# Moving the softmax sums, the place bases and the first weight splits of a fused attention and mixture-of-experts kernel

## The chip, the cores and the metric

The kernel runs on one core of a Trainium2 chip. The metric is the device time of one execution in microseconds (us), lower is better; for a kernel it is the median of several runs. The engines are PE (TensorE: matmuls and transposes, with PEld its weight loads), DVE (VectorE), ACT (ScalarE), POOL (GpSimd) and SP (SyncE, which only issues transfers). Each takes its own instructions strictly in the order in which the program lists them, and engines wait for one another by semaphores.

## What is computed

Causal attention with a window of 64 over q, k, v of shape (8, 8, 576, 64), and then a mixture of eight experts, of which each token takes one, over the 4608 rows of 512 that it gives:

```python
scores = scale * np.matmul(q, k.transpose(0, 1, 3, 2))          # scale = 1/sqrt(64)
mask = (rel >= 0) & (rel < 64)                                   # rel = query - key
attn = np.exp(np.where(mask, scores, -1e9) - max)
attn = attn / (np.sum(attn, axis=-1, keepdims=True) + 1e-09)
x = (attn @ v) as rows of (B * S, H * D)                         # 4608 x 512
logits = normalized(x) @ normalized(expert_emb).T / tau
expert_idx = np.argmax(logits, axis=1)
gate_w = softmax(logits)[expert_idx]
out[mask_e] = gate_w * (np.maximum(x[mask_e] @ w1[e], 0.0) @ w2[e])   # for each of 8 experts
```

## The kernel before

The program has a manual schedule: instructions are issued in the order in which the Python code is written, and no scheduler moves them. It has three stretches.

**Attention, stages 0 to 34.** The tokens are 36 tiles of 128 rows. `stages(s)` (L520) is one turn of a software pipeline: it computes the scores of tile s, the weighted values of tile s - 2 and the routing of tile s - 3. In one turn PE does `scores(s)` (L215), for groups of four tiles that end three tiles back also `logits_four` (L351), then `values_other(s-2)` (L275) into the only PSUM tile `pair`, `attn_transposes(s-1)` (L245), `x_transposes(s-3)` (L331), at some turns `ranks` (L412 to L416), and `values_mine(s-2)` (L289), which completes `pair`. ACT copies scores (`own_scores`, L222), the turned attention (`attn_copy`, L255) and the turned x (`xT_evac`, L337) out of PSUM, squares x with an accumulator (`squares`, L324), triggers the load of a k tile (L176) and takes the exponentials (L236). DVE masks the scores (`all_scores`, L225), takes maxima (L229), masks the turned attention (`attn_prev`, L258), and then runs `x_out` (L309): it adds 1e-9 to the row sums in `pair` (L313), inverts them (L314) and multiplies the 512 columns of `pair` by them into x (L315). Only then is `pair` free, so the next turn's L275 waits for L315. POOL subtracts the maxima (L233), masks the other half of the attention (L261) and scatters finished rows of x into a DRAM table sorted by expert (`place`, L462).

At some turns DVE also routes a group. `choose(G)` (L382) has five small operations on the group's logits, which ACT has copied out of PSUM into the rows of x (`four_out`, L361). `ranks(G)` counts on PE, in PSUM, how many earlier tokens took the same expert; `rank_rows(G)` (L440) then adds each expert's base in the table (L445), masks by the choice (L447), sums (L450) and casts (L453) to give each token's row in the table.

**The first expert's weights.** Matmuls of the expert layers run as three products of two-part numbers (a high part and the rest), so w1 and w2 are split: ACT makes the high part and DVE the rest. During attention the first expert's w1 is loaded in eight halves (`wsteps`, stages 8 to 28) and split in eight halves (`wsplit`, stages 13 to 32, L600 on ACT and L601 on DVE, at the end of the stage). After stages 32 and 33 `x_parts` prepares the first two slots of 128 table rows for that expert: four 32-column turns on DVE (L770), the high part on ACT (L781), the rest on POOL (L785). Their loads (L755) are issued after stage 30.

**The mixed stretch and the experts.** After stage 34 the last tile's attention is woven by hand with the first expert's first layer (L887). Tile 35's parts are called one by one (L1091 to L1211). Then DVE computes from the counts which expert each slot of rows belongs to (`slot_rows`), and `step(g)` runs one slot group after another: layer 1 (L887), layer 2 (L947), splits of the next weights (L158, L161), scatter of results (L959).

Of the kernel before, what the change touches and what calls it, by code (L numbers as in the profile page):

```python
# [9 lines left out]
F32 = mybir.dt.float32  # L10
# [73 lines left out]
def attention_moe(ctx, tc, q, k, v, emb, tau, w1, w2, kc, kt, out):  # L84
# [56 lines left out]
    upper = const.tile([P, P], BF16, name="upper")  # L141
    ones = const.tile([P, P], BF16, name="ones")
    half = const.tile([P, 1], F32, name="half")
    embT = ap.tile([P, 4, 32], F32, name="embT", bufs=1)
    xs = dram.tile([TBL, ROW], F32, name="xs")

# [27 lines left out]
    def load_k(T, engine=nc.sync):  # L174
        if T < NT:
            engine.dma_start(kT[:, T % RK * KT:(T % RK + 1) * KT], k[T])  # L176
# [43 lines left out]
    def own_scores(T):  # L220
        sm[T] = ap.tile([P, 4, 2, WIN], F32, name="sm", bufs=3)
        nc.scalar.copy(sm[T], sv[:, :, :, 1])  # L222
# [12 lines left out]
    def exponentials(T):  # L235
        nc.scalar.activation(sm[T], sm[T], AF.Exp, scale=0.125)  # L236
# [65 lines left out]
    def x_rows(a, b):  # L302

        if a // 4 in (2, 5):
            return xmore[:, a % 4:a % 4 + b - a]
        i = a if a < 8 else a - 12 if a < 20 else a - 24 if a < 34 else a - 34
        return xall[:, i:i + b - a]

    def x_out(T):  # L309
        t = xr[T] = x_rows(T, T + 1)[:, 0]  # L310
        p4 = px.pop(T)[:, :, :4 * (D + 1)].rearrange("p b (h d) -> p b h d", h=4)
        sums = ap.tile([P, 2, 2, 4], F32, name="sums")
        nc.vector.tensor_scalar(out=sums[:, 0], in0=p4[:, :, :, D], scalar1=1e-9, scalar2=None, op0=ALU.add)  # L313
        nc.vector.reciprocal(sums[:, 1], sums[:, 0])  # L314
        nc.vector.tensor_tensor(out=t[:, :DM].rearrange("p (b c d) -> p b c d", b=2, c=4), in0=p4[:, :, :, :D],  # L315
                                in1=sums[:, 1].unsqueeze(3).to_broadcast([P, 2, 4, D]), op=ALU.mult)
# [55 lines left out]
    def in_rows(G):  # L372

        return x_rows(*GROUPS[G])[:, :, C_LOG:C_LOG + E]
# [6 lines left out]

    def choose(G):  # L382

        L = in_rows(G)
        a, b = GROUPS[G]
        n = b - a
        m = ap.tile([P, n, 1], F32, name="m")
        c8 = ap.tile([P, n, E], F32, name="c8")
        oh = ohs[G] = ap.tile([P, n, E], BF16, name="oh")
        sh = [P, n, E]  # L390
        nc.vector.reduce_max(out=m, in_=L, axis=AX.X)
        nc.vector.tensor_tensor(out=c8, in0=L, in1=m.to_broadcast(sh), op=ALU.is_equal)
        nc.vector.tensor_tensor(out=c8, in0=c8, in1=cs[:, K_DESC:K_DESC + E].unsqueeze(1).to_broadcast(sh), op=ALU.mult)
        nc.vector.reduce_max(out=m, in_=c8, axis=AX.X)
        nc.vector.tensor_tensor(out=oh, in0=c8, in1=m.to_broadcast(sh), op=ALU.is_equal)
# [11 lines left out]
    def ranks(G):  # L407

        a, b = GROUPS[G]
        n = b - a  # L410
        rank[G] = rkb[0][:, 64:128].rearrange("p (a g e) -> p a g e", a=2, e=E)[:, G % 2, :n]
        nc.tensor.matmul(rank[G], lhsT=upper, rhs=ohs[G], start=True, stop=False)  # L412
        for i in range(1, n):
            nc.tensor.matmul(rank[G][:, i:], lhsT=ones, rhs=ohs[G][:, i - 1:i].to_broadcast([P, n - i, E]), start=False, stop=False)
        for i in range(4):
            nc.tensor.matmul(rank[G], lhsT=ones, rhs=before[G][:, i:i + 1].to_broadcast([P, n, E]), start=False, stop=i == 3)  # L416

    late = [const.tile([P, E], F32, name=f"late{i}") for i in range(len(CUTS))]
    shift = [const.tile([P, 1], F32, name=f"shift{i}") for i in range(len(CUTS))]
# [20 lines left out]
    def rank_rows(G):  # L440
        a, b = GROUPS[G]
        n = b - a
        rk = ap.tile([P, n, E], F32, name="rk")
        at = [cs[:, K_E:K_E + E], *late][sum(a >= cut for cut in CUTS)]
        nc.vector.tensor_tensor(out=rk, in0=rank.pop(G), in1=at.unsqueeze(1).to_broadcast([P, n, E]), op=ALU.add)  # L445
        yield
        nc.vector.tensor_tensor(out=rk, in0=rk, in1=ohs.pop(G), op=ALU.mult)  # L447
        yield
        pos = ap.tile([P, n], F32, name="pos")
        nc.vector.reduce_sum(out=pos, in_=rk, axis=AX.X)  # L450
        yield
        rks[G] = ap.tile([P, n], I32, name="pi")
        nc.vector.tensor_copy(rks[G], pos)  # L453
        yield
# [47 lines left out]


    wsteps = {}
    for i, s0 in enumerate((8, 10, 15, 18, 21, 24, 26, 28)):
        c, h = divmod(i, 2)
        at = slice(h * 512, (h + 1) * 512)
        wsteps.setdefault(s0, []).append(lambda c=c, at=at: nc.sync.dma_start(out=w1raw[c][:, at], in_=w1v[0, :, c, at]))

    for i, s0 in enumerate((29, 30, 30, 31, 31, 32, 32, 33)):  # L510
        c, h = divmod(i, 2)
        wsteps.setdefault(s0, []).append(lambda c=c, h=h: nc.sync.dma_start(out=w2raw[c][:, h], in_=w2v[0, :, c, h]))
    wsplit = {s0: (i // 2, slice(i % 2 * 512, i % 2 * 512 + 512)) for i, s0 in enumerate((13, 15, 20, 23, 26, 28, 30, 32))}

    def warm(n, to=back):

# [3 lines left out]
    def stages(s):  # L520

        def there(d):
            return 0 <= s - d < NT

        def ending(d):
            return [G for G, (a, b) in enumerate(GROUPS) if b + d == s]
# [7 lines left out]
        if s < 3:  # L534
            warm(12, misc)
        own_scores(s)
        if there(4) and s - 4 >= 28:
            logits(s - 4)
        four = [G for G in ending(3) if len(range(*GROUPS[G])) == 4]
# [33 lines left out]
        if there(3):  # L573
            squares(s - 3)
        load_k(s + RK - 1, nc.scalar)
        if s > 3:
            attn_prev(s - 1)
            attn_own(s - 1)
        if there(2):
            x_out(s - 2)  # L580
        if 0 < s <= 3:
            turned()
            attn_prev(s - 1)
            attn_own(s - 1)
# [4 lines left out]
        for G, (a, b) in enumerate(GROUPS):  # L589
            for T in range(a, b):  # L590
                if s == (T + 9 if b - a == 4 else b + 4):
                    place(T)
        for G in ending(3):
            choose(G)
            tokens(G)
            count(G)
        exponentials(s)
        if s in wsplit:
            c, at = wsplit[s]
            nc.scalar.copy(w1h[c][:, at], w1raw[c][:, at])  # L600
            nc.vector.tensor_tensor(out=w1l[c][:, at], in0=w1raw[c][:, at], in1=w1h[c][:, at].bitcast(F32), op=ALU.subtract)  # L601
# [449 lines left out]
    nc.vector.memset(ones, 1.0)  # L1051
    nc.vector.memset(low, -BIG / 64)
    nc.vector.memset(half, 0.5)
    nc.scalar.copy(shift[0], half)
    nc.vector.memset(embT, 0.0)
    nc.vector.memset(before[0], 0.0)
# [10 lines left out]
    for t in range(NT - 1):  # L1067
        stages(t)
        if t == 0:
            nc.vector.tensor_copy(upper, xbuf[2][:, :P])  # L1070
        if t == 1:
            expert_norms()
        if t == 2:
            expert_emb()
        if t == 3:
            expert_emb_T()
        if t == CUTS[0] + 4:
            sum_counts(CUTS[0])
            begin_late(0, counts("early"))
        if t == 30:  # L1080
            load_x(0)
            load_x(1)
        if t in (32, 33):
            x_parts(t - 32)

    stage_t.close()
    rkb[0] = misc
# [206 lines left out]
```

## Time and profile before

| what | value |
|---|---|
| median of 3 runs | 628.08 us (627.51 to 628.99) |
| the profiled execution's own time | 623.06 us |
| its span, first to last instruction | 621.3 us |
| granted TensorE clock, mean | 0.994 |
| PE, PEld busy | 594.8 us (96%), 530.9 us (85%) |
| DVE, ACT, POOL busy | 426.9, 354.9, 231.4 us |
| the same, 100 to 120 us (attention): PE, DVE, ACT, POOL of 20 us | 17.24, 17.72, 13.22, 15.81 |
| the same, 240 to 260 us (experts) | 20.00, 13.38, 12.60, 5.50 |

Rows of a timeline read: start in us, duration in us, engine, line, operation, output<-inputs, count, and in brackets how long the engine had been idle before and which instruction ended that. Rows of groups read: line, engine, operation, tiles, shape, count | busy us, mean ns of one | idle before, and who ended it. A queue name such as SPq or ACTq is the engine's issue of a transfer, not busy time.

### The profile page before, as it was taken

The page shows a single profiled execution, that of the slowest core. Times are in us where ns is not written, and L with a number is a line of the kernel's source. Part 1 is how long each engine was busy: PE and PEld are TensorE (multiplying, and loading weights), DVE is VectorE, ACT ScalarE, POOL GpSimd, SP SyncE. Part 2 cuts the span into 40 slices and gives each one's busy share as a digit, 9 for nine tenths or more (in the row PEclk, how much of TensorE's full clock was granted, in tenths as well). Part 3 has the DMA queues.
Part 4 walks back from the last instruction along what each step waited for, and adds up shares of the span by engine and source line. Part 5 has one row for each costly group of instructions (what it writes and reads, how often), then busy time and mean ns, then how long its engine had stood idle before and what let it go on. Part 6 is the DMA issues. An engine that isn't in the chain of part 4 may idle for free. (4 is left out here: it accounts for less than half of the span.)

```text
span 621.3 us, 17783 instructions
## 1 busy us (share of the span) xinstructions
PE 594.8 (96%) x6836; PEld 530.9 (85%) x6836; DVE 426.9 (69%) x883; ACT 354.9 (57%) x566; POOL 231.4 (37%) x224
## 2 busy tenths in 40 slices
PE   8899989888999999999999999999999999999996
PEld 8777777777899898989988999899889998998884
DVE  2778888887778657675566776656765677657623
ACT  2676766676542447466466664645676476636533
POOL 1567877778733133213203331142023331222011
PEclk9999999999899999999999999999999999999998
DMA  8878888886335588886786897849777976775351
GB/s 293 263 208 256 259 264 270 266 273 186 151 115 204 137 271 279 255 257 227 250 269 219 273 299 245 258 157 324 252 242 240 283 275 206 241 273 199 111 167 37
DMA packets 85789, 143.75 MB, mean 231 GB/s; under 512 B 15797, under 2 KB 36021, under 8 KB 85696
## 3 DMA queue, kind: packets, MB, share of 16 engines
q1 hardware_dynamic: 74560, 112.87, 58.5%
q0 software_dynamic: 6000, 19.18, 7.8%
q10 hardware_dynamic: 5136, 10.49, 5.0%
q8 instruction: 55, 0.90, 0.6%
q14 instruction: 38, 0.31, 0.2%
HBM read 123.23 MB, written 20.05 MB: 231 GB/s over the span
## 5 line engine op out<-in xcount | busy, mean ns | idle before, releaser
L887 PE MATMUL ph<-xh,w1l 128*128 128x256 f32 x576 | 162.3, 282 | 1.0 <-DVE w1l L161 1.0
L887 PE MATMUL ph<-xh,w1h 128*128 128x256 f32 x576 | 162.4, 282 | 0.0
L887 PE MATMUL ph<-xl,w1h 128*128 128x256 f32 x576 | 161.7, 281 | 0.0
L959 POOL DMA_INDIRECT out<-o,rest x39 | 49.4, 1266 | 220.4 <-ACT o L956 204.8
L947 PE MATMUL po<-w2h,hh 128*128 128x512 f32 x312 | 122.3, 392 | 0.0
L947 PE MATMUL po<-w2h,hl 128*128 128x512 f32 x312 | 121.9, 391 | 0.0
L947 PE MATMUL po<-w2l,hh 128*128 128x512 f32 x312 | 121.7, 390 | 0.0
L901 DVE SCALAR_TENSOR_TENSOR hl<-ph,hh 128x512 fp32r<-128x512 f32 x78 | 53.4, 689 | 93.0 <-ACT hh L897 92.9
L161 DVE TENSOR_TENSOR w2l<-w2raw,w2h 128x1024 fp32r<-128x1024 f32 x80 | 94.7, 1220 | 24.6 <-ACT w2h L158 22.9
L887 PEld LDWEIGHTS ph<-xh,w1l 128*128 128x128 f32 x576 | 108.4, 188 | 1.6 <-DVE w1l L161 1.4
L887 PEld LDWEIGHTS ph<-xl,w1h 128*128 128x128 f32 x576 | 108.6, 188 | 0.8
L887 PEld LDWEIGHTS ph<-xh,w1h 128*128 128x128 f32 x576 | 108.2, 188 | 0.8
L158 ACT CAST w2h<-w2raw 128x1024 fp32r<-128x1024 f32 x80 | 81.5, 1048 | 40.0 <-PE po L947 28.7
L161 DVE TENSOR_TENSOR w1l<-w1raw,w1h 128x1024 fp32r<-128x1024 f32 x76 | 89.2, 1236 | 11.0 <-ACT w1h L158 11.0
L785 POOL TENSOR_TENSOR xl<-xt,xh 128x512 fp32r<-128x512 f32 x37 | 47.8, 1293 | 101.2 <-ACT xh L781 101.2
L897 ACT ACTIVATE hh<-ph 128x512 fp32r<-128x512 f32 x78 | 46.1, 595 | 57.2 <-PE ph L887 50.6
L158 ACT CAST w1h<-w1raw 128x1024 fp32r<-128x1024 f32 x76 | 73.9, 1047 | 0.0
L947 PEld LDWEIGHTS po<-w2h,hl 128*128 128x128 f32 x312 | 58.6, 188 | 12.5
L947 PEld LDWEIGHTS po<-w2h,hh 128*128 128x128 f32 x312 | 58.6, 188 | 11.5
L947 PEld LDWEIGHTS po<-w2l,hh 128*128 128x128 f32 x312 | 58.6, 188 | 11.4
L781 ACT CAST xh<-xt 128x512 fp32r<-128x512 f32 x39 | 24.2, 620 | 57.4 <-DVE xt L770 56.6
L233 POOL TENSOR_TENSOR sm<-sm,st 128x512 f32<-128x512 f32 x36 | 37.4, 1040 | 37.8 <-DVE st L229 29.8
(194 smaller groups left out, 834.5 us busy)
## 6 DMA issues: line engine op xcount, KB each, us to landing
w2raw<-in_w SPq DMA_DIRECT2D x76, 512.0 KB, 5.8
w1raw<-in_w SPq DMA_DIRECT2D x72, 512.0 KB, 4.7
xb<-xs SPq DMA_DIRECT2D x156, 64.0 KB, 6.2
v<-in_v SPq DMA_DIRECT2D x36, 260.0 KB, 4.2
qT<-in_q SPq DMA_DIRECT2D x36, 256.0 KB, 4.1
kT<-in_k ACTq DMA_DIRECT2D x32, 256.0 KB, 4.1
w1raw<-in_w SPq DMA_DIRECT2D x8, 256.0 KB, 4.3
w2raw<-in_w SPq DMA_DIRECT2D x8, 256.0 KB, 4.7
```

What stands on the lines that cost most here:

```text
L158: nc.scalar.copy(hi[c], raw[c])
L161: eng.tensor_tensor(out=lo[c], in0=raw[c], in1=hi[c].bitcast(F32), op=ALU.subtract)
L233: nc.gpsimd.tensor_tensor(out=t, in0=t, in1=st.pop(T).unsqueeze(2).to_broadcast([P, 8, WIN]), op=ALU.subtract)
L781: nc.scalar.copy(xh, t)
L785: eng.tensor_tensor(out=xl, in0=t, in1=xh.bitcast(F32), op=ALU.subtract)
L887: nc.tensor.matmul(o, lhsT=ww[c][:, f * P:(f + 1) * P], rhs=xx[:, c, :n], start=(c == 0 and i == 0), stop=(c == 3 and i == 2))
L897: nc.scalar.activation(hh, ph[g, part], AF.Relu)
L901: nc.vector.scalar_tensor_tensor(out=hl, in0=ph.pop((g, part)), scalar=0.0, in1=hh.bitcast(F32), op0=ALU.max, op1=ALU.subtract)
L947: nc.tensor.matmul(po[a], lhsT=xx[:, f, at], rhs=ww[f // 2][:, f % 2], start=(f == 0 and i == 0), stop=(f == 7 and i == 2))
L959: d = nc.gpsimd.indirect_dma_start(out=out, out_offset=bass.IndirectOffsetOnAxis(ap=tok, axis=0), in_=o, in_offset=None, bounds_check=N - ...
```

## The change

1. **Sums on ACT.** The addition of 1e-9 to the eight row sums of a tile (L313 on DVE) becomes an ACT activation, `Identity` with a bias read from a constant [128, 1] tile. In the stages it is listed on ACT behind `squares` and the k load, ahead of the exponentials; DVE keeps the inversion and the multiplication. For tiles 33 to 35, in the mixed stretch, it is listed where `x_out` is called.
2. **Bases on PE.** The experts' bases are added by one more matmul at the end of `ranks`, a single row of ones (fp32) against the bases. `rank_rows` loses its addition; its mask now reads PSUM.
3. **Choice from PSUM.** For groups of four, `choose` reads the logits from PSUM instead of the copy in the rows of x. The copy is still made, since the rows carry it.
4. **Even steps.** The eight w1 loads move to stages 8, 10, 12, 15, 17, 19, 21, 23 and the splits to 14, 16, ..., 28.
5. **Turned x.** The two `x_parts` after stages 32 and 33 are taken apart and put inside those stages.

```diff
+    def x_sums(T):
+        sums = sums_of[T] = ap.tile([P, 2, 2, 4], F32, name="sums")
+        p4 = px[T][:, :, :4 * (D + 1)].rearrange("p b (h d) -> p b h d", h=4)
+        nc.scalar.activation(sums[:, 0], p4[:, :, :, D], AF.Identity, bias=tiny)
+
     def x_out(T):
+        if T not in sums_of:
+            x_sums(T)
+        sums = sums_of.pop(T)
...
-        nc.vector.tensor_scalar(out=sums[:, 0], in0=p4[:, :, :, D], scalar1=1e-9, scalar2=None, op0=ALU.add)
         nc.vector.reciprocal(sums[:, 1], sums[:, 0])
...
     def choose(G):
-        L = in_rows(G)
+        L = plq[:, G % 2, :, :E] if n == 4 else in_rows(G)
...
     def ranks(G):
         for i in range(4):
-            nc.tensor.matmul(rank[G], lhsT=ones, rhs=before[G][:, i:i + 1].to_broadcast([P, n, E]), start=False, stop=i == 3)
+            nc.tensor.matmul(rank[G], lhsT=ones, rhs=before[G][:, i:i + 1].to_broadcast([P, n, E]), start=False, stop=False)
+        at = [cs[:, K_E:K_E + E], *late][sum(a >= cut for cut in CUTS)]
+        nc.tensor.matmul(rank[G], lhsT=one, rhs=at[:1].unsqueeze(1).to_broadcast([1, n, E]), start=False, stop=True)
...
     def rank_rows(G):
-        nc.vector.tensor_tensor(out=rk, in0=rank.pop(G), in1=at.unsqueeze(1).to_broadcast([P, n, E]), op=ALU.add)
-        yield
-        nc.vector.tensor_tensor(out=rk, in0=rk, in1=ohs.pop(G), op=ALU.mult)
+        nc.vector.tensor_tensor(out=rk, in0=rank.pop(G), in1=ohs.pop(G), op=ALU.mult)
...
-    for i, s0 in enumerate((8, 10, 15, 18, 21, 24, 26, 28)):
+    for i, s0 in enumerate((8, 10, 12, 15, 17, 19, 21, 23)):
...
-    wsplit = {s0: (i // 2, slice(i % 2 * 512, i % 2 * 512 + 512)) for i, s0 in enumerate((13, 15, 20, 23, 26, 28, 30, 32))}
+    wsplit = {s0: (i // 2, slice(i % 2 * 512, i % 2 * 512 + 512)) for i, s0 in enumerate((14, 16, 18, 20, 22, 24, 26, 28))}
...
     def stages(s):
         own_scores(s)
+        if s == 33:
+            x_hi(0)
...
         load_k(s + RK - 1, nc.scalar)
+        if there(2):
+            x_sums(s - 2)
...
         if there(2):
             x_out(s - 2)
+        if s in (32, 33):
+            x_turned(s - 32)
...
+        if s == 33:
+            x_lo(0)
         for G in ending(3):
             choose(G)
...
         exponentials(s)
+        if s == 33:
+            x_hi(1)
+            x_lo(1)
...
-        if t in (32, 33):
-            x_parts(t - 32)
```

How the instructions move, on the engines and at the places that matter below. First ACT in a stage in the middle of the attention: `score`, `back` and `xback` are the PSUM tiles of scores, turned attention and turned x, `sq` the discarded squares, `sm` the scores in SBUF. Before:

```order
L337 COPY xfour<-xback 128x512
L324 ACTIVATE sq,xmore<-xmore 128x512
L176 DMA kT<-in_k 128x512
L236 ACTIVATE sm<-sm 128x512
L222 COPY sm<-score 128x512
```

and in the changed kernel:

```order
L347 COPY xfour<-xback 128x512
L334 ACTIVATE sq,xr<-xr 128x512
L178 DMA kT<-in_k 128x512
L316 ACTIVATE sums<-pair,tiny 128x8
L238 ACTIVATE sm<-sm 128x512
L224 COPY sm<-score 128x512
```

The sums, which read `pair`, now stand on ACT between the k load and the exponentials, in each of the stages.

Second, DVE in stage 32 and the start of stage 33, where the first turned x (`xt`) is made. Before:

```order
L313 TENSOR_SCALAR sums<-pair 128x8
L314 RECIPROCAL sums<-sums 128x8
L315 TENSOR_TENSOR xr<-pair,sums 128x512
L601 TENSOR_TENSOR w1l_112<-w1raw,w1h_108 128x512
L770 STREAM_TRANSPOSE xt_224<-xb_218 128x4x32 x4
L225 COPY_PREDICATED sm<-cs,score 128x512
```

and now:

```order
L325 TENSOR_TENSOR xr<-pair,sums 128x512
L790 STREAM_TRANSPOSE xt_228<-xb_222 128x4x32 x4
L227 COPY_PREDICATED sm<-cs,score 128x512
L231 TENSOR_REDUCE st<-sm 128x8
L260 TENSOR_TENSOR aM<-back,cs 128x512
L324 RECIPROCAL sums<-sums 128x8
L325 TENSOR_TENSOR xr<-pair,sums 128x512
L790 STREAM_TRANSPOSE xt_229<-xb_223 128x4x32 x4
L456 TENSOR_TENSOR rk<-rkb,oh 128x32
```

The split is gone from stage 32, and the second tile's turns stand ahead of the stage's rank and choice operations instead of behind them.

Third, ACT around the last tile's output in the mixed stretch (`hh` is the first expert's hidden layer, `w2h` the high part of its w2). Before:

```order
L337 COPY xT<-back 128x512
L324 ACTIVATE sq,xr<-xr 128x512
L897 ACTIVATE hh_3369<-ph_3416 128x512
L158 CAST w2h_3363<-w2raw_103 128x1024
L337 COPY xT<-back 128x512
```

and now:

```order
L347 COPY xT<-back 128x512
L334 ACTIVATE sq,xr<-xr 128x512
L917 ACTIVATE hh_3373<-ph_3420 128x512
L160 CAST w2h_3367<-w2raw_105 128x1024
L316 ACTIVATE sums<-pair,tiny 128x8
L347 COPY xT<-back 128x512
```

The last tile's sums stand behind a cast of 1024 columns.

More of the change, by code (lines that the diff above doesn't have):

```diff
@@ L143, in attention_moe @@
     half = const.tile([P, 1], F32, name="half")
+    tiny = const.tile([P, 1], F32, name="tiny")
+    one = const.tile([1, P], F32, name="one")
     embT = ap.tile([P, 4, 32], F32, name="embT", bufs=1)
@@ L307, in x_rows @@
         return xall[:, i:i + b - a]
+    sums_of = {}
+    def x_sums(T):
+        sums = sums_of[T] = ap.tile([P, 2, 2, 4], F32, name="sums")
+        p4 = px[T][:, :, :4 * (D + 1)].rearrange("p b (h d) -> p b h d", h=4)
+        nc.scalar.activation(sums[:, 0], p4[:, :, :, D], AF.Identity, bias=tiny)
     def x_out(T):
+        if T not in sums_of:
+            x_sums(T)
+        sums = sums_of.pop(T)
         t = xr[T] = x_rows(T, T + 1)[:, 0]
         p4 = px.pop(T)[:, :, :4 * (D + 1)].rearrange("p b (h d) -> p b h d", h=4)
-        sums = ap.tile([P, 2, 2, 4], F32, name="sums")
-        nc.vector.tensor_scalar(out=sums[:, 0], in0=p4[:, :, :, D], scalar1=1e-9, scalar2=None, op0=ALU.add)
         nc.vector.reciprocal(sums[:, 1], sums[:, 0])
@@ L443, in rank_rows @@
         rk = ap.tile([P, n, E], F32, name="rk")
-        at = [cs[:, K_E:K_E + E], *late][sum(a >= cut for cut in CUTS)]
-        nc.vector.tensor_tensor(out=rk, in0=rank.pop(G), in1=at.unsqueeze(1).to_broadcast([P, n, E]), op=ALU.add)
-        yield
-        nc.vector.tensor_tensor(out=rk, in0=rk, in1=ohs.pop(G), op=ALU.mult)
+        nc.vector.tensor_tensor(out=rk, in0=rank.pop(G), in1=ohs.pop(G), op=ALU.mult)
         yield
@@ L1053, in attention_moe @@
     nc.vector.memset(half, 0.5)
+    nc.vector.memset(tiny, 1e-9)
+    nc.vector.memset(one, 1.0)
     nc.scalar.copy(shift[0], half)
```

## The prediction

> **What bounds the kernel now.** I read the 20 us stretches first, because the share of busy time mixes two regimes, and then what PE waited for in each.
>
> ```profile
> 100.00:120.00 20.00, 17.24 (x492) 14.66 (x484) 17.72 (x46) 13.22 (x31) 15.81 (x16) 1.00 0.83 270
> 240.00:260.00 20.00, 20.00 (x127) 18.08 (x126) 13.38 (x20) 12.60 (x16) 5.50 (x5) 1.00 0.79 241
> PE pair L275 <- DVE xr L315: 9.9, 17, 1.3
> PE ph L887 <- DVE w1l L161: 1.0, 2, 0.5
> ```
>
> The columns after each stretch are PE, PEld, DVE, ACT and POOL. The experts (second row) are bound by PE, which never pauses; after 160 us its largest sum of waits is the last row, 1.0 us in two pieces. So whatever the change saves ahead of 163 us, when the first expert layer starts, should arrive at the end, and PE time added later is paid in full. In attention no engine is full; PE waits above all (third row, up to 160 us) for the multiplication L315, which frees `pair`. I therefore follow one stage (17) from L275 to the next L275.
>
> ```profile
> 80.31 0.70 PE L275 MATMUL pair<-v,aM 64*64 64x65 f32 x32 [1.32 <-DVE xr L315]
> 80.91 0.73 DVE L225 COPY_PREDICATED sm<-cs,score 128x512 f32<-128x512 uint32 x1 [0.66 <-ACT sm L222]
> 81.97 0.25 PE L416 MATMUL rkb<-before,ones 128*128 128x32 bf16 x4
> 82.16 1.05 PE L289 MATMUL pair<-v,aM 64*128 64x65 f32 x24
> 82.21 0.33 ACTq L176 DMA_DIRECT2D kT<-in_k  x1
> 82.35 0.68 DVE L258 TENSOR_TENSOR aM<-back,cs 128x512 f32<-128x512 f32 x1
> 82.59 0.64 ACT L324 ACTIVATE sq<-xr 128x512 bf16<-128x512 f32 x1
> 83.12 0.20 ACT L324 ACTIVATION_READ_ACCUMULATOR sq<-xr 128x1 f32 x1
> 83.28 0.17 DVE L313 TENSOR_SCALAR sums<-pair 128x8 f32<-128x8 f32 x1 [0.24 <-PE pair L289]
> 83.48 0.20 DVE L314 RECIPROCAL sums<-sums 128x8 f32<-128x8 f32 x1
> 83.72 0.69 DVE L315 TENSOR_TENSOR xr<-pair,sums 128x512 f32<-128x512 f32 x1
> 84.33 0.18 DVE L445 TENSOR_TENSOR rk<-rkb,cs 128x32 f32<-128x32 f32 x1
> 84.46 0.70 PE L275 MATMUL pair<-v,aM 64*64 64x65 f32 x32 [0.38 <-DVE xr L315]
> 88.98 0.70 PE L275 MATMUL pair<-v,aM 64*64 64x65 f32 x32
> 93.05 0.68 PE L275 MATMUL pair<-v,aM 64*64 64x65 f32 x16 [0.38 <-DVE xr L315]
> 97.14 0.46 PE L275 MATMUL pair<-v,aM 64*64 64x65 f32 x16 [0.74 <-DVE xr L315]
> ```
>
> PE needs 2.90 us from L275 to the end of L289 (83.21); then come addition, inversion and multiplication, and L275 follows at 4.15. This round, through PE and DVE, sets the stage. Stage 18 takes 4.52 without a wait: PE has a group's logits to do before L275, and is itself the limit. Stages 19 and 20 take 4.07 and 4.09. The four make 16.83 us. Stages with a split or a blocked choice are longer:
>
> ```profile
> 29.16 0.70 PE L275 MATMUL pair<-v,aM 64*64 64x65 f32 x32 [0.38 <-DVE xr L315]
> 150.65 0.70 PE L275 MATMUL pair<-v,aM 64*64 64x65 f32 x32 [0.37 <-DVE xr L315]
> L447 DVE TENSOR_TENSOR rk<-rk,oh 128x32 f32<-128x32 f32 x7 | 3.3, 476 | 0.2
> ```
>
> The first two rows are 28 stages (5 to 33) apart: 121.5 us, against 7 x 16.83 = 117.8. So late DVE work costs some 3.7 us now. That is all that relieving DVE can win here.
>
> **The change part by part: the stages.** DVE loses L313 (0.20 from its start to the next) in every stage, and for every group L445 (0.21). L447, 476 ns on average, becomes an operation with one input from PSUM, like L445's 0.18, though it does the same work on the same shape; it is one with both inputs in SBUF that is long. The Trainium skill (SBUF — State Buffer, Who interferes with whom) says that a `tensor_tensor` with both inputs in SBUF contends with GpSimd's reads; the trace agrees, 0.48 against 0.18. In `choose`, though, the operation behind the one that now reads PSUM has two SBUF inputs (L393) and would inherit the block, so I count nothing for it. DVE's round (multiplication to next operation 0.61, L225 to L258 1.44, L258 0.68, inversion 0.24) is then 2.97 us; with five choice operations, each 0.20 to 0.24 like L313 and L314, it is 4.1, with a split (0.69, row below) 3.7. None is above the 4.15, and with splits in even stages and choices in odd ones they never add up. So rounds of PE, and of ACT, cover DVE's, and I take its lateness as gone; were the cover away, up to the 3.7 us would be.
>
> But ACT's answer comes later than DVE's would. ACT's accumulator read, behind the copies and the squares, starts 2.81 us after L275 (83.12). What the sums cost follows from these rows of groups and of the last tile:
>
> ```profile
> L897 ACT ACTIVATE hh<-ph 128x512 fp32r<-128x512 f32 x78 | 46.1, 595 | 57.2 <-PE ph L887 50.6 <-PE ph L933 6.3
> L956 ACT ACTIVATE o<-po,gate 128x512 f32<-128x512 f32 x38 | 24.0, 681 | 0.9 <-DVE gate L844 0.7 <-ACTq L1031 0.2
> L545 ACT COPY xr<-misc 128x16 f32<-128x16 f32 x1 | 0.2, 175 | 0.0
> 181.33 0.19 ACT L324 ACTIVATION_READ_ACCUMULATOR sq<-xr 128x1 f32 x1
> 181.42 0.59 ACT L897 ACTIVATE hh<-ph 128x512 fp32r<-128x512 f32 x1
> 181.90 1.04 ACT L158 CAST w2h<-w2raw 128x1024 fp32r<-128x1024 f32 x1
> 181.96 0.17 DVE L313 TENSOR_SCALAR sums<-pair 128x8 f32<-128x8 f32 x1 [1.13 <-PE pair L289]
> 183.50 0.49 PE L331 MATMUL back<-cs,xr 128*128 128x128 f32 x3
> ```
>
> The instruction behind an accumulator read starts 0.09 after it. A small copy from PSUM takes 175 ns; an activation with an operand per partition (L956's scale; the sums' bias is of that kind) takes 86 ns more than one without (L897). I take 0.26 us, between 0.175 and 0.29. So the sums end 2.81 + 0.09 + 0.26 = 3.16 after L275, the inversion starts at 3.19, the multiplication 0.24 later, L275 0.74 after that: 4.17 for a plain stage, 4.26 where ACT also copies a group's logits (one small instruction, 0.09 like the one above). In rank stages PE is last: 2.90, plus the new matmul, plus 0.03 + 0.26 + 0.03 + 0.24 + 0.74. The matmul is not in the trace; the nearest row is L416, four bf16 ones in 0.25 together, the later ones some 0.03 apart. A single row of fp32 could cost anything from one such step, 0.03, to as much as all four, 0.25; I take 0.12, the middle. That makes 4.32. The stage with logits stays at 4.52. Four stages: 17.27; 28: 120.9, of which I take off 0.1, as two meet an edge of a sequence and are shorter on PE. **Term 1: 120.8 - 121.5 = -0.7 us.** The sums alone would cost 0.4 us per four stages; it is DVE's punctuality that pays. Behind the sums on ACT stand the exponentials, and behind these the next score copy, for which DVE waits; but the exponentials wait for POOL's subtraction in any case.
>
> The Trainium skill (ScalarE: Activation LUTs, What ACT_TABLE_LOAD costs) gives 93 ns for a pointer operand and 280 ns plus 0.833 ns per element for such an activation: an estimate of 0.29 us, by which term 1 would shrink by about 0.6. The trace's 86 ns agrees with the 93.
>
> **The last two stages.** Here the present order stalls:
>
> ```profile
> 151.29 0.69 DVE L601 TENSOR_TENSOR w1l<-w1raw,w1h 128x512 fp32r<-128x512 f32 x1 [0.69 <-ACT w1h L600]
> 151.90 0.88 DVE L770 STREAM_TRANSPOSE xt<-xb 128x128 f32<-128x128 f32 x4
> 152.81 0.62 ACT L781 CAST xh<-xt 128x512 fp32r<-128x512 f32 x1 [1.56 <-DVE xt L770]
> 157.16 0.39 PE L275 MATMUL pair<-v,aM 64*64 64x65 f32 x4 [0.75 <-DVE xr L315]
> 159.08 1.02 POOL L462 DMA_INDIRECT xs<-xr,pi  x1 [1.25 <-issue]
> 160.83 1.27 POOL L785 TENSOR_TENSOR xl<-xt,xh 128x512 fp32r<-128x512 f32 x1 [0.23 <-ACT xh L781]
> 163.23 0.39 PE L887 MATMUL ph<-xh,w1h 128*128 128x256 f32 x1
> ```
>
> Split, turns and high part follow one another, the next score copy (L222) stands behind them on ACT, and L275 of stage 34 comes 6.51 after that of stage 33 (150.65). In the change no split stands there, the copy comes first and the turns directly follow the multiplication, so I give this stage the 4.25 of its neighbours: -2.25. From there to the first layer is 6.07 now. Then: multiplication 0.74 before L275, turns from -0.13 to 0.77, three rank operations to 1.4, the scatter (with 0.15 issue) to 2.55, the first rest (1.27) to 3.8, counters (three small ones) 0.4, the second rest to 5.5. PE's own way there is shorter: choice to 2.5, masking 0.73 and the scores behind it. That is -0.55. **Term 2: -2.8 us.** The cover is the load of the first slot, which DVE's turns wait for; if it lands late, DVE stands still and with it the masking and maxima behind.
>
> **The last tile.** Its sums stand behind the cast of 1.04: they start at 182.85 instead of 181.96, the inversion at 183.14 instead of 182.16, and L331, which PE reaches at 183.40 to 183.50, waits until 184.1. **Term 3: +0.7.** For tiles 33 and 34 they stand right behind the squares; behind them waits the hidden layer's high part (L897), whose reader on DVE comes later still, and I count nothing. Three rank calls lie in PE's full stretch: **term 4: 3 x 0.12 = +0.4.** The sum is -0.7 - 2.8 + 0.7 + 0.4 = -2.4 us: 623.06 becomes 620.7. The median of the runs is 5.0 us above the profiled execution; the same difference gives **625.7**. The unknown prices: the sums at 0.175 or 0.29 in the 21 stages not held at 4.52 move it by -1.8 or +0.6, the matmul, ten times on the path, by -0.9 or +1.3.
>
> **Rivals.** *ACT's queue makes it slower.* The k trigger (L176, 0.33) stands between squares and sums. In the rows above it starts 0.38 before the squares do, so it runs ahead. If it or the wait for PE holds the sums up instead, 21 stages lengthen by 0.33, +6.9, and the time is 632.6; from 0.11 us per stage on the change loses. For it: ACT would become the last engine in most stages, which it is in none now. The Trainium skill (ScalarE: Activation LUTs, Rules for kernel authors) advises additions on VectorE, not ScalarE, and so stands on this side; the rows have 0.16 to 0.17 for L313 against my 0.26. Chance 0.17. *The end of attention gives little:* the load lands late, or the two rests on POOL are held up by DVE, and of term 2 only 0.8 stays: 627.7. The load's issue and its time to landing:
>
> ```profile
> 145.68 4.31 SPq L755 DMA_DIRECT2D xb<-xs  x8
> xb<-xs SPq DMA_DIRECT2D x8, 64.0 KB, 2.7
> ```
>
> The eight parts of both slots are issued in 4.31 us from 145.68 on; the first slot's four are out at about 147.8 and, with 2.7, there at 150.5; the turns now want it at 150.6. Chance 0.18. *The stages keep their short rounds:* the sums come no later than now, 16.83 per four stages, term 1 is -3.7, the time 622.7. Against it: ACT's copies, squares and read are one chain. Chance 0.13.
>
> **How the numbers follow.** My forecast has 0.52, its own range 624.2 to 627.2. About 0.2% (1.26 us) is what a measurement tells from no change, so faster means below 626.8. Faster: 0.44 of the forecast, all of the third rival and a little of the second, 0.60. Same: the rest of these two, 0.23. Slower: 0.17. The range 622.4 to 629.5 leaves out the full price of the slow rival and little else.
>
> **What would show it.** Right: L314 3.2 us after L275 in plain stages, never earlier, behind ACT; L275 to L275 near 4.17, 4.32, 4.52, 4.25 with no 4.9 or 5.1 left; stage 33 to 34 below 4.5; a pause of PE before L331 of the last tile. Wrong: DVE still late at L314, rounds above 4.4 without a split, L770 waiting for a transfer, or a first layer that begins earlier while the end does not.

## The result

The changed kernel takes 634.68 us (median; 632.97 to 638.41) against 628.56 for the kernel before on the same chip: a ratio of 1.0097, 95% interval 1.0071 to 1.0122. It is slower by 6 us, where 2.4 us less were forecast. Most lines have moved: L275, L245, L255, L289, L314, L315 and L324 of the kernel before are L277, L247, L257, L291, L324, L325 and L334 now; the sums are L316, the new matmul is L428.

The kernel before was profiled once more (run before_again below), because its first profiled execution, 623.06 us, lies under every timed run. The second one took 627.51. It has nearly the same stages (122.4 us instead of 121.5 for the 28), but pauses in the last tiles that the first did not have, as two rows of its timeline show (start, duration, engine and line):

```profile
167.41 0.99 PE L275 MATMUL pair<-v,aM 64*64 64x65 f32 x30
168.83 0.32 PE L275 MATMUL pair<-v,aM 64*64 64x65 f32 x2 [0.43 <-issue]
```

The value step of the third last tile is broken by a pause in which PE waits for nothing that the profile shows ("issue"). I compare the changed kernel with this second profile; the granted clock of the two executions was 0.999 and 0.994. From the timeline of the changed kernel, the values of stages 33 and 34 and the first expert layer:

```profile
159.59 0.69 PE L277 MATMUL pair<-v,aM 64*64 64x65 f32 x31 [0.19 <-issue]
...
164.37 0.70 PE L277 MATMUL pair<-v,aM 64*64 64x65 f32 x32
...
168.74 0.38 PE L907 MATMUL ph<-xh,w1h 128*128 128x256 f32 x1
```

| start, us | before, first profile | before, second profile | changed | changed less second |
|---|---|---|---|---|
| values of stage 5 | 29.16 | 28.17 | 29.98 | +1.8 |
| values of stage 33 | 150.65 | 150.59 | 159.59 | +9.0 |
| values of stage 34 | 157.16 | 157.10 | 164.37 | +7.3 |
| first expert layer | 163.23 | 163.17 | 168.74 | +5.6 |
| fifth copy of a hidden part | 195.91 | 199.81 | 207.70 | +7.9 |
| span | 621.3 | 625.7 | 632.9 | +7.2 |

From the last copy on, all three run in step. So the 28 stages from 5 to 33 lose 7.2 us, the last two stages give 3.4 back, and the last tiles lose 2.3. The 1.8 ahead of stage 5 I leave aside: it comes and goes between kernels that are alike there (low_early reaches stage 5 in 13.7 us from stage 2, low_base in 16.5). It lies in stage 3, which takes 4.8 to 6.8 us in the eight profiles with the sums on ACT and 4.8 to 6.3 in the nine with them on DVE, so a part of it may be the change's.

A plain stage (5) of the changed kernel, on the timeline:

```profile
29.98 0.70 PE L277 MATMUL pair<-v,aM 64*64 64x65 f32 x32 [0.77 <-ACT sm L224]
30.71 0.34 SPq L182 DMA_DIRECT2D v<-in_v  x1
31.30 0.59 ACT L257 COPY aM<-back 128x512 f32<-128x512 f32 x1 [1.44 <-PE back L247]
...
32.79 0.20 ACT L334 ACTIVATION_READ_ACCUMULATOR sq<-xr 128x1 f32 x1
32.88 0.27 ACT L316 ACTIVATE sums<-pair,tiny 128x8 f32<-128x8 f32 x1
33.18 0.20 DVE L324 RECIPROCAL sums<-sums 128x8 f32<-128x8 f32 x1 [0.50 <-ACT sums L316]
33.49 0.69 DVE L325 TENSOR_TENSOR xr<-pair,sums 128x512 f32<-128x512 f32 x1
34.33 0.29 PE L277 MATMUL pair<-v,aM 64*64 64x65 f32 x4 [0.77 <-ACT sm L224]
```

Up to the inversion it is as forecast: accumulator read 2.81 after L277, sums at 2.90, inversion at 3.20. Then the multiplication comes 0.31 later instead of 0.24, and L277 another 0.84 instead of 0.74: 4.35, not 4.17. A stage with a group's ranks (13):

```profile
65.99 0.70 PE L277 MATMUL pair<-v,aM 64*64 64x65 f32 x32 [0.78 <-DVE xmore L325]
...
66.42 1.02 POOL L471 DMA_INDIRECT xs<-xr,pi  x1
66.61 0.66 PE L247 MATMUL back<-cs,sm 128*128 128x128 f32 x4
...
67.82 0.33 SPq L182 DMA_DIRECT2D v<-in_v  x1
67.83 0.40 PE L428 MATMUL rkb<-cs,one 1*128 1x32 f32 x2
67.90 0.59 ACT L257 COPY aM<-back 128x512 f32<-128x512 f32 x1 [1.72 <-PE xback L341]
68.16 1.05 PE L291 MATMUL pair<-v,aM 64*128 64x65 f32 x24
...
69.48 0.27 ACT L316 ACTIVATE sums<-pair,tiny 128x8 f32<-128x8 f32 x1
...
70.93 0.27 PE L277 MATMUL pair<-v,aM 64*64 64x65 f32 x2 [0.70 <-DVE rk L456]
```

Here three things are new. L291 starts 2.17 after L277, against 1.85 (82.16 - 80.31) in stage 17 before: the new matmul, two passes of a row of fp32, adds 0.32. The copy L257 starts at 67.90, although L247, whose output it reads, ended at 67.27; and the load of v, which waits for L277 and goes 0.73 after its start in stage 5, goes at 1.83. PE itself ran on all the while: what came late is the news of its work. The trace records when PE's semaphore is raised: after the start of L277 no raise is on record until 67.80, and then three within 0.14 us, while DVE's semaphore is raised at 66.96 and 67.75, right at the ends of its operations. ACT's squares and sums stand behind the late copy, so the sums start at 3.49 instead of 2.90. A scatter of POOL (L471) runs over the end of L277.

### The profile page after: what moved, and what is told of

The parts are those of the page before. It is cut to its first block, busy times and chain, and to the rows that moved or that the text cites. A ratio compares the mean times of both kernels' runs of the same rounds, so it can differ in the third digit from the quotient of the medians.

```text
span 632.9 us, 17858 instructions
## 1 busy us (share of the span) xinstructions
PE 597.5 (94%) x6858; PEld 533.3 (84%) x6858; DVE 420.3 (66%) x838; ACT 359.9 (57%) x602; POOL 232.4 (37%) x224
## 5 line engine op out<-in xcount | busy, mean ns | idle before, releaser
L967 PE MATMUL po<-w2h,hl 128*128 128x512 f32 x312 | 121.8, 390 | 0.0
```

The costliest lines, as they stand in the source:

```text
L967: nc.tensor.matmul(po[a], lhsT=xx[:, f, at], rhs=ww[f // 2][:, f % 2], start=(f == 0 and i == 0), stop=(f == 7 and i == 2))
```

## The experiments

**One part taken back at a time.** Four kernels with the changed one as the start.

```diff
 sums_dve: in x_sums, which only x_out calls now
-        nc.scalar.activation(sums[:, 0], p4[:, :, :, D], AF.Identity, bias=tiny)
+        nc.vector.tensor_scalar(out=sums[:, 0], in0=p4[:, :, :, D], scalar1=1e-9, scalar2=None, op0=ALU.add)
 base_dve: in ranks and rank_rows
-        nc.tensor.matmul(rank[G], lhsT=one, rhs=at[:1]..., start=False, stop=True)
-        nc.vector.tensor_tensor(out=rk, in0=rank.pop(G), in1=ohs.pop(G), op=ALU.mult)
+        nc.vector.tensor_tensor(out=rk, in0=rank.pop(G), in1=at..., op=ALU.add)
+        nc.vector.tensor_tensor(out=rk, in0=rk, in1=ohs.pop(G), op=ALU.mult)
 choice_sbuf: in choose
-        L = plq[:, G % 2, :, :E] if n == 4 else in_rows(G)
+        L = in_rows(G)
 moves_only: all three
```

> The change with its sums put back on DVE, into x_out (L313 as before); place bases, choice and moves stay as changed. Theory S (the sums on ACT, with the two waits that they add ahead of the multiplication and ahead of L277, are most of the loss): some 5 us less than the changed kernel, about 1.001 of the time before; plain stages back at 4.1 or less, and the own copy of the weights (L257) back at 1.3 us after L277 in the stages with ranks or four logits. Rival R (the rank matmul and the choice from PSUM are the loss): at most 1.5 us less, 1.007 to 1.010, with stages 11, 13 and 15 still near 4.9.

> The change with the place bases added by DVE again (no L428); sums, choice and moves stay as changed. Theory S: the matmul costs its 0.32 us only in the seven or so stages where the rank sums stand between the two value steps, so some 2 us less than the changed kernel: 1.006 to 1.007 of the time before; L291 starts at 1.85 after L277 instead of 2.17. Rival R: 4 us less or more, 1.003.

> The change with the choice reading its logits from the rows in SBUF again; sums, bases and moves stay as changed. Theory S: no more than 1 us either way, 1.008 to 1.011 of the time before: what DVE is late by is hidden behind ACT's sums. Rival R (DVE's reads of PSUM hold up PE's logits and the copies behind them): 3 us less, 1.005, with L257 back at 1.3 us after L277.

> The kernel before with the even splits and the moved turns alone; sums, bases and choice as before. Theory S: the gain of the last two stages arrives, 2 to 4 us less than before, 0.994 to 0.997; stage 33 below 4.8. Rival: the two rests on POOL and the later turns give it back behind the last stage, 0.999 to 1.001.

Measured: sums_dve 0.9987 (0.9972 to 1.0002), base_dve 1.0140 (1.0103 to 1.0177), choice_sbuf 1.0076 (1.0055 to 1.0098), moves_only 0.9981 (0.9965 to 0.9998) of the time before. Theory S holds where it matters: with the sums back on DVE the loss is gone, some 7 us, and the plain stage 5 is back at 3.95. Other expectations of it do not hold. In sums_dve the copy L257 is late too (1.98 after L277 in stage 13). Taking the matmul away brings no 2 us. The higher median of base_dve is no price of DVE's two operations either: the granted clock of its six runs is 0.981 to 0.997, the lower it is the longer they take, and the run at 0.997 takes 633.96, as the changed kernel does at 0.999 (632.97 to 634.64, in another session). In its profile, whose stages 5 to 33 take 131.4 us, the granted clock is 0.50 from 158 to 160, in stage 32, which takes 5.62 against 4.34 in the changed kernel. So with the sums on ACT the runs do not tell the matmul and DVE's two operations apart. With sums on DVE the matmul does cost its 0.33 in stages 9 and 13 (4.48 against 4.15 in moves_only). The choice from PSUM is no clear gain or loss. Groups of instructions in the changed kernel (total, mean ns, idle before them):

```profile
L316 ACT ACTIVATE sums<-pair,tiny 128x8 f32<-128x8 f32 x36 | 9.7, 270 | 6.4 <-PE pair L291 4.1 <-DMA qT<-in_q 2.3
L379 PE MATMUL misc<-embT,xT 128*64 128x8 f32 x128 | 5.1, 205 | 1.6 <-DVE c L402 1.5
L428 PE MATMUL rkb<-cs,one 1*128 1x32 f32 x10 | 2.0, 282 | 0.0
L402 DVE TENSOR_TENSOR c<-misc,m 128x32 f32<-128x32 f32 x7 | 1.3, 191 | 0.2
```

The comparison in the choice (L402) takes 191 ns from PSUM; in choice_sbuf, from SBUF, 192, though it reads SBUF as in the kernel before, where it took 438 to 652 ns (first profile); that with the sums on ACT it comes at a time when POOL is not at work is inferred. In exchange PE's logits (L379) wait 1.5 us once, in stage 31, for DVE's read of the same PSUM tile; that stage takes 5.78, in choice_sbuf 4.89. And moves_only is hardly faster than the kernel before: its stages 5 to 33 take 123.4 us, against 121.5 and 122.4 in the two profiles of before.

**The sums alone, and what in them costs.**

```diff
 sums_only: the kernel before, and only
+        if there(2):
+            x_sums(s - 2)            # ACT, behind squares and the k load
 sums_only_nowait, sums_nowait (the latter: in the changed kernel)
+    tc.declare_no_dep(m, sums, ...)             # each value matmul m behind the sums
+    tc.declare_no_dep(multiplication, m, ...)   # the multiplication behind each matmul m
 sums_first_nowait: as sums_only_nowait, and
+        if there(2):
+            x_sums(s - 2)            # ahead of the squares
         if there(3):
             squares(s - 3)
         load_k(s + RK - 1, nc.scalar)
```

Both orders that are declared away follow from the chain values, sums, inversion, multiplication. In the traces an instruction carries at most one wait, and further ones stand in semaphore instructions ahead of it: in sums_only the trace has 90 of these on PE instead of 63 before, and 366 on DVE instead of 352; in sums_only_nowait 63 and 352 again.

> The kernel before with the sums on ACT and nothing else. Theory S (they cost this in any surrounding): about 1.010 of the time before, plain stages 4.35, stage 3 near 5.2 or more. Rival (they are dear only together with the rank matmul and the moved splits): 1.003 or less.

> The changed kernel without the two waits that the sums on ACT add: L277 waits for DVE's multiplication alone, not for ACT too, and the multiplication for the inversion alone, not for PE too (both orders follow from the chain values, sums, inversion, multiplication). Theory W (each added wait is an instruction of its own and costs 0.06 to 0.1 us in the round): plain stages go from 4.35 to 4.17, those with ranks or four logits lose as much, those held by PE at 4.52 stay: some 3 us less than the changed kernel, 1.004 to 1.006 of the time before. Rival (the place of the sums behind the squares costs it all): 1.008 to 1.010, plain stages still 4.3.

> The kernel before with the sums on ACT alone, and without the two waits that they add (L277 for ACT, the multiplication for PE). Theory W (a good part of the sums' price is the added waits): plain stages 4.17 instead of 4.35, about 1.007 of the time before, against 1.0114 with the waits. Rival (their price is the place behind squares and accumulator read alone): 1.010 or more.

> As the run before it, and the sums stand ahead of the squares in ACT's queue instead of behind them. Theory Q (the rest of the price is the place in ACT's queue: they could start at 2.72 us after L277 instead of 2.90): plain stages near 4.05, 1.000 to 1.004 of the time before. Rival (ACT then waits for PE with the squares, exponentials and the next score copy behind it): the copy L224 comes 0.7 later, DVE with it, 1.008 or more.

Measured: sums_only 1.0114 (1.0084 to 1.0145); sums_nowait 1.0064 (1.0037 to 1.0091); sums_only_nowait 1.0055 (1.0031 to 1.0080); sums_first_nowait 0.9985 (0.9970 to 1.0000). The sums alone cost what the whole change costs. In the kernel before, leaving out the waits takes half of it away, and the other place the rest; in the changed kernel plain stages shrink as well (stage 5: 4.19 instead of 4.35), but the interval of sums_nowait still meets that of the changed kernel. The granted clock was alike in the three kernels with the sums alone, 0.990 to 0.991 on average. Stage 8 of sums_only, of sums_only_nowait and of sums_first_nowait, on the timeline (in the latter two L277, L316, L324 and L325 are L280, L325, L333 and L334):

```profile
47.02 0.20 DVE L324 RECIPROCAL sums<-sums 128x8 f32<-128x8 f32 x1 [0.33 <-ACT sums L316]
...
47.32 0.69 DVE L325 TENSOR_TENSOR xr<-pair,sums 128x512 f32<-128x512 f32 x1
...
48.16 0.35 PE L277 MATMUL pair<-v,aM 64*64 64x65 f32 x9 [0.77 <-DVE xr L325]
```

```profile
45.34 0.20 DVE L333 RECIPROCAL sums<-sums 128x8 f32<-128x8 f32 x1 [0.23 <-ACT sums L325]
45.58 0.69 DVE L334 TENSOR_TENSOR xr<-pair,sums 128x512 f32<-128x512 f32 x1
...
46.32 0.39 PE L280 MATMUL pair<-v,aM 64*64 64x65 f32 x10 [0.61 <-DVE xr L334]
```

```profile
41.49 0.70 PE L280 MATMUL pair<-v,aM 64*64 64x65 f32 x32 [0.48 <-DVE xr L334]
...
44.27 0.27 ACT L325 ACTIVATE sums<-pair,tiny 128x8 f32<-128x8 f32 x1 [0.38 <-PE pair L297]
...
45.55 0.57 PE L280 MATMUL pair<-v,aM 64*64 64x65 f32 x22 [0.47 <-DVE xr L334]
```

From inversion to multiplication 0.30 with the wait, 0.24 without; from there to the values 0.84 and 0.74: 0.16 us of round for two waits that order nothing. Ahead of the squares the sums start 2.78 after the values instead of 2.90; the stage takes 4.35, 4.18 and 4.06. But plain stages alone do not make the difference: stages 5 to 33 take 128.9, 126.7 and 121.8 us, and most of the last 4.9 lies in stages 12, 13, 15, 19, 23 and 27, where L257 is late in sums_only_nowait (1.75 to 2.06) and, but for stage 19, at 1.32 to 1.37 in sums_first_nowait. The price that the rival set on it, a score copy 0.7 later, did not come.

**The late copy and the scatter.** In the profiles so far, with few exceptions, L257 was late where a scatter had started while L277 ran (0.70 us long), and on time where it started after L277's end. Where it was late by much, it went 1.3 to 1.7 us after the scatter's start (in the changed kernel 1.64 in stage 15, scatter at 0.02, and 1.91 in stage 13, scatter at 0.44). In the first profile of the kernel before, 11 of the 23 stages from 11 to 33 have the scatter just behind that end, at 0.81 to 0.84, as stage 17, whose values start at 80.31:

```profile
79.70 1.27 POOL L261 TENSOR_TENSOR aM<-aM,cs 128x512 f32<-128x512 f32 x1
81.13 1.01 POOL L462 DMA_INDIRECT xs<-xr,pi  x1 [0.15 <-issue]
```

POOL's own masking ends 0.66 after the values' start, and the scatter starts at 0.82.

```diff
 scatter_after (changed kernel), scatter_moves (moves_only): in stages
+        if 10 <= s <= 34:
+            place(s - 10)            # between less_max and attn_own on POOL
-                if s == (T + 9 if b - a == 4 else b + 4):
+                if s == b + 4 and b - a == 2 or s == 34 and T == 25:
 low_delay: low_early (below), and ahead of place(T) for groups of four
+                        for i in range(2):
+                            nc.gpsimd.tensor_copy(idle[:, 32 * i:32 * i + 32], idle[:, 64:96])
```

> The changed kernel with each scatter of a group of four on POOL one place later in its queue, between the subtraction of the maxima (L235) and the next own masking (L263), so that none runs while L277 ends. Theory P (PE's semaphore updates are held back while a scatter runs over the end of L277, and the copy L257 with them): L257 back at 1.32 us after L277 in stages 11 to 31, ten stages shorter by up to 0.5: 3 to 5 us less than the changed kernel, 1.001 to 1.005 of the time before. Rival (the rank matmul or the logits themselves hold the copy up): L257 stays at 1.7 to 1.9, 1.008 or more; later masking could even make it slower.

> The kernel with the moves alone, with each scatter of a group of four between L235 and the next own masking. Theory P: L257 back at 1.32 us after L277 in stages 15 to 31; the 28 stages 5 to 33 take 121.5 or less instead of 123.4; 0.995 to 0.997 of the time before. Rival (the splits in even stages make DVE late and this delays the copy): L257 still near 2.0, 0.998.

Measured: 1.0336 (1.0305 to 1.0366) and 1.0313 (1.0282 to 1.0344), some 20 us slower than before. In scatter_moves the copy is back at 1.32 in stages 16 to 26, but something larger takes its place, as two groups of scatter_moves and the same two of moves_only show:

```profile
L622 DVE TENSOR_TENSOR w1l<-w1raw,w1h 128x512 fp32r<-128x512 f32 x8 | 14.7, 1831 | 5.5 <-ACT w1h L621 4.8 <-ACT sm L238 0.7
L457 DVE TENSOR_TENSOR rk<-rk,oh 128x32 f32<-128x32 f32 (+1 forms) x11 | 12.2, 1113 | 0.3
```

```profile
L457 DVE TENSOR_TENSOR rk<-rk,oh 128x32 f32<-128x32 f32 (+1 forms) x11 | 6.6, 600 | 0.3
L620 DVE TENSOR_TENSOR w1l<-w1raw,w1h 128x512 fp32r<-128x512 f32 x8 | 5.5, 692 | 4.6 <-ACT w1h L619 4.6
```

The scatter pushes POOL's masking under DVE's operations with two inputs in SBUF, and these end only after POOL's has: 1.83 us for a split instead of 0.69. The Trainium skill (SBUF — State Buffer, Who interferes with whom) names this contention; the trace agrees, by 1.14 us per split. So this pair said nothing clean on the late copy, and a smaller step was needed: low_delay moves the scatter by two small copies alone.

> The kernel with the early rest (0.995 of the time before), with two small copies on POOL (some 0.15 us each) ahead of each scatter of a group of four, so that scatters which started 0.5 to 0.7 us after L277 start after its end at 0.70. Theory P (PE's semaphore updates, and the copy L257 with them, are held back when a scatter runs over the end of L277): L257 back at 1.32 in stages 13, 19, 23, 27, 28, 31 and 33, where it stood at 2.0, these stages shorter by up to 0.4: 0.990 to 0.994 of the time before. Rival (the lateness belongs to these stages, not to the scatter's start): L257 stays at 2.0, no gain or a loss of some 0.3 per stage.

Measured: 0.9939 (0.9920 to 0.9959), the fastest of all. Stage 27 of low_early and of low_delay (in the latter L277, L247, L182, L257 and L472 are L278, L248, L183, L258 and L473):

```profile
125.24 0.70 PE L277 MATMUL pair<-v,aM 64*64 64x65 f32 x32
125.74 1.37 POOL L472 DMA_INDIRECT xs<-xr,pi  x1 [0.17 <-issue]
125.86 0.66 PE L247 MATMUL back<-cs,sm 128*128 128x128 f32 x4
127.17 0.33 SPq L182 DMA_DIRECT2D v<-in_v  x1
127.25 0.59 ACT L257 COPY aM<-back 128x512 f32<-128x512 f32 x1 [1.09 <-PE misc L368]
```

```profile
123.90 0.70 PE L278 MATMUL pair<-v,aM 64*64 64x65 f32 x32
...
124.64 0.33 SPq L183 DMA_DIRECT2D v<-in_v  x1
125.12 1.02 POOL L473 DMA_INDIRECT xs<-xr,pi  x1 [0.15 <-issue]
125.22 0.58 ACT L258 COPY aM<-back 128x512 f32<-128x512 f32 x1 [0.46 <-PE back L248]
...
88.92 0.70 PE L278 MATMUL pair<-v,aM 64*64 64x65 f32 x32
...
89.47 1.02 POOL L473 DMA_INDIRECT xs<-xmore,pi  x1 [0.16 <-issue]
...
90.93 0.58 ACT L258 COPY aM<-back 128x512 f32<-128x512 f32 x1 [1.60 <-PE misc L369]
```

With the scatter 1.22 after the values instead of 0.50, v's load goes at 0.74 instead of 1.93 and the copy at 1.32 instead of 2.01. In stages 12, 13, 15, 23, 27, 28, 31 and 32, late in low_early, it is on time; stage 33 is at 1.57, behind ACT's own earlier work, and the two stages that stay late are those where the scatter still starts inside the values: stage 19 (last three rows, 0.55) and stage 24 (0.65). Stages 5 to 33 take 121.5 us instead of 123.5; 0.5 of that is lost again between stage 34 and the first layer. That putting the scatter off brings the copy back is shown. Why PE's signals are held up by it is not, and it does not happen always: in the first profile of before, scatters that started at 0.30, 0.55 and 0.64 did not delay the copy. In the second the one at 0.55 did. And in low_early the copies of stages 12 and 15 are late by 0.8 behind scatters at 0.76 and 0.74, just after L277's end, so the edge is not sharp.

**The moves.**

```diff
 turned_only: the kernel before with the moved turns, wsplit and wsteps as before
 low_early: turned_only, and
-        if s == 33:
-            x_lo(0)                  # behind the scatters
+        if s == 33:
+            x_lo(0)                  # ahead of less_max(33)
 low_base: low_early, and the bases by TensorE for groups of two alone
 before_again: the kernel before, unchanged
```

> The kernel before with the moved turns and parts of x alone; the splits stay in their old stages. Theory E (the even splits bring nothing: the 28 stages were 1.9 us longer with them): 121.5 for stages 5 to 33, and 1 to 2 us less than with all moves, 0.994 to 0.997 of the time before. Rival (the even splits save what the prediction said of DVE's lateness): 0.999 to 1.003.

> The kernel with the turns moved (old splits), with the first slot's rest on POOL (x_lo(0)) ahead of the subtraction of the maxima of stage 33, where POOL stands still for 1.23 us. Theory B (what the moved turns gain is given back because DVE's rank product, L457, with both inputs in SBUF, stands 2.95 us behind POOL's unbroken work, against 0.66 before): POOL's run is shorter by 1.27, PE waits less for the second rest, some 1.5 to 3 us less than with the turns alone: 0.993 to 0.996 of the time before. Rival (PE's work in the last tiles is what counts): 0.998.

> As the run with the early rest, and for the groups of two alone the place bases are added by TensorE, so that their rank product reads PSUM. Theory B: L456's product takes 0.17 instead of up to 2.95, at most 1 us for the three matmuls on PE and perhaps the next operation blocked in its place: 0.991 to 0.996. Rival: the block falls on the next operation with its data in SBUF, no gain over the early rest alone.

> The kernel before, unchanged, profiled once more, since its profiled execution (623.06 us) lies below every timed run (627.51 to 633.4). Theory N (the profile that the prediction was made against is an execution some 5 us shorter than the usual one, shorter within attention): the ratio is 1.000, and this profile shows a span near 626, with 2 to 5 us more ahead of the first expert layer or in the last tiles than the first profile. Rival (profiled executions are always shorter): span 621 to 622 again.

Measured: turned_only 0.9978 (0.9956 to 1.0000), low_early 0.9948 (0.9928 to 0.9967), low_base 0.9961 (0.9943 to 0.9979), before_again 1.0001 (0.9981 to 1.0020). Splits in even stages bring nothing: without them the moves are as fast as with them. The turns do gain ahead of the first layer, which starts at 160.11 in turned_only (163.17 before), but most of it is lost right behind, as the rows of turned_only and then of low_early show:

```profile
160.66 1.25 POOL L804 TENSOR_TENSOR xl<-xt,xh 128x512 fp32r<-128x512 f32 x1
161.24 2.95 DVE L457 TENSOR_TENSOR rk<-rk,oh 128x16 f32<-128x16 f32 x1
...
161.97 0.41 PE L906 MATMUL ph<-xl,w1h 128*128 128x256 f32 x1 [1.47 <-POOL xl L804]
```

```profile
161.71 0.39 PE L906 MATMUL ph<-xl,w1h 128*128 128x256 f32 x1 [0.25 <-POOL xl L804]
...
162.22 1.71 DVE L457 TENSOR_TENSOR rk<-rk,oh 128x16 f32<-128x16 f32 x1
```

PE's first layer waits 1.47 us for the second rest on POOL, and DVE's rank product stands under POOL's unbroken work for 2.95. With the first rest in the gap that POOL had in stage 33, both shrink, and 3 us remain as a gain. How much of turned_only's loss is POOL's is open: in its profile the granted clock is also about 0.50 from 162 to 168, in low_early's it is 1.00 there, and over the runs it is 0.989 to 0.997 against 0.996 to 0.999. The gain itself is not the clock's alone: three runs of low_early at 0.996 and 0.997 that took longest need 626.91 to 627.61, while no run of the kernel before at 0.996 or more in that session is under 628.2. The matmul for the last groups adds nothing to it. Three versions, low_early, low_base and low_delay, beat both kernels clearly; moves_only lies under the kernel before by a hair.

## Why the prediction was wrong

**The step that failed is term 1, the stages:** -0.7 forecast, +7.2 measured against the second profile (129.6 against 122.4). It failed in four places.

- *What the sums cost in a round.* The operation was priced well, 0.26 against 0.270 (the Trainium skill's page, ScalarE: Activation LUTs, What ACT_TABLE_LOAD costs, gives an estimate of 0.29; the trace is nearer to the row than to it), and so was its start. What was left out are the waits: I carried "0.24 later, L275 0.74 after that" over from a chain that ran through DVE and PE alone. A third engine in the chain adds a wait to the multiplication and one to L277, 0.16 us together in the run above, and sums_only_nowait against sums_only is 1.0055 against 1.0114.
- *"DVE's punctuality pays."* The 3.7 us of lateness were taken as gone. The even splits, meant to bring it, brought nothing (turned_only against moves_only).
- *The stages as rounds of PE, DVE and ACT.* The sum left POOL's scatters out. In the kernel before they start some 0.82 after the values in about half of the stages, 0.12 behind the end of L277; a round that grows by some tenths while POOL's work does not brings their start ahead of that end, and the copy comes up to 0.7 late. That putting the scatter off brings the copy back is shown by low_delay; that this edge is the larger part of the sums' price is inferred, from the stages in which the other place in ACT's queue saves its 4.9 us.
- *The matmul,* taken at 0.12 with 0.25 as the upper bound, delays L291 by 0.32. The bound from four bf16 matmuls did not hold for fp32, which shows as two passes. It is a small error: 0.20 in each of the six rank stages of this stretch, 1.2 us at most.

**Term 2, the last two stages,** was right in kind and low in size: stage 33 takes 4.78 instead of 6.51 (4.25 forecast), and the first layer starts 4.37 after it instead of 6.07 (5.5 forecast): -3.4 for -2.8. The cover named for it held: the turns did not wait for the first slot's load. What gives part of the gain back in turned_only and moves_only is PE's wait for the second rest at the end of POOL's unbroken work (1.47 us in both), which the prediction had only touched in a rival.

**Terms 3 and 4** together were +1.1; the last tiles lose 2.3 from the first layer on. No run splits that, but the trace of the changed kernel shows two parts. The last tile's sums do stand behind the cast, at 192.61, and L341 starts 0.77 later behind L426 than L331 did behind L416 (0.7 forecast); but the new matmul takes 0.39 of that on PE, so terms 3 and 4 overlap here and PE pauses for 0.21. The other part was in no term: right behind the first layer PE waits 1.20 us for the second rest on POOL, and meanwhile DVE stands in a small operation:

```profile
169.28 0.16 DVE L456 TENSOR_TENSOR rk<-rkb,oh 128x16 f32<-128x16 f32 x1
169.68 2.86 DVE L462 CAST pi<-pos 128x2 int32<-128x2 f32 x1
```

The rank product, which now reads PSUM, is short, as forecast; but the cast two operations later, from SBUF to SBUF, takes 2.86 us beside POOL's work, against 0.17 on average in its three other places. The prediction saw that a block would move on in `choose`, and did not ask it of `rank_rows`.

**The offset of 5.0 us** between profile and median was right as a sum, but it was no constant of the measurement: the first profile had no pause of PE in the last tiles, the second has. A row like "its largest sum of waits is 1.0 us" held for that execution only.

**The rival that ACT's queue makes it slower** gave 632.6, near the 634.7, by the wrong mechanism. The k trigger ran ahead of the squares as forecast and never held the sums up. But its general part stood: ACT became the last engine of the round. The rule of the Trainium skill on that side (ScalarE: Activation LUTs, Rules for kernel authors: additions on VectorE) would have given the right sign; the runs put 7 us beside it, but not for the operation itself, 0.270 against 0.17 us: in sums_first_nowait it is on ACT too, and the kernel takes 0.9985 of the time before.

## What to carry to other kernels

Moving a small operation from the engine that waits anyway to a third one adds waits on both sides of it, even where the order already follows; count these (here 0.06 and 0.10 us) and see if they can be declared away. A stage that looks like a round of two engines can sit on an edge set by another one, here 0.12 us between the end of a matmul group and the start of a scatter: look at what starts just after the path's events before making the round longer. Take a second profile of the kernel before, if the first lies outside the timed runs. And look at the granted clock before reading a difference of 1%: the higher median of base_dve went with it.

## What was unexpected in the hardware

- Around the time in which POOL issues an indirect scatter, what waits for PE's signals can be held up: a load and a copy that wait for matmuls ended at 0.70 and 1.29 after the start of a stage went at 1.93 and 2.01 (stage 27 of low_early), with PE itself running on. It showed, with few exceptions, for scatters that started before the end of the first of these matmul groups, and the copy then went 1.3 to 1.7 us after the scatter's start.
- Two small copies on POOL that only put the scatter off made the kernel some 1.4 us faster by medians, 624.90 against 626.34 in two sessions; their intervals against the kernel before, 0.9920 to 0.9959 and 0.9928 to 0.9967, overlap, so this last step is likely rather than sure.
- DVE's subtraction with both inputs in SBUF took 1.83 us instead of 0.69 under POOL's masking, and a cast of 128x2 took 2.86 instead of 0.17 beside POOL's work.
